# Sliding-window attention gated with a token-mixing MLP: column-tiled PV for nine more query tiles, V weights earlier in the load queue, first x block in halves, last output split, order of instructions tuned anew

## The chip, the cores and the metric

The kernel runs on one core of one Trainium2 chip. Times are device microseconds (us) of one execution. A run is 1.7 to 2.1 us longer than the span that the record gives for it. The program uses one core, so there is no second die to compare with. A run counts as slow when it is over 1.5% above the fastest run of the same kernel, and comparisons use the other runs, called fast.

PE is TensorE (its matmuls), DVE is VectorE, ACT is ScalarE, POOL is GpSimd, and SP is the engine that does nothing here but issue the DMAs.

## The reference

```python
def _A_ref(x, wqkv, wo):                    # x: 1 x 2048 x 512, H = 32 heads of 16, window W = 256
    q, k, v = split_heads(x @ wqkv)
    scores = einsum("bhqd,bhkd->bhqk", q, k) * Dh ** -0.5
    mask = (qi - ki >= 0) & (qi - ki < W)
    p = softmax(where(mask, scores, -1e9))
    return merge_heads(einsum("bhqk,bhkd->bhqd", p, v)) @ wo

def _B_ref(x, w1, b1, w2, b2):              # the MLP mixes along the sequence: S = 2048, F = 1376
    u = gelu(einsum("bsd,sf->bdf", layernorm(x), w1) + b1)
    return (einsum("bdf,fs->bds", u, w2) + b2).transpose(0, 2, 1)

g = sigmoid((x * gate_w).sum(-1, keepdims=True))
return g * _A_ref(x, wqkv, wo) + (1 - g) * _B_ref(x, w1, b1, w2, b2)
```

Everything is bfloat16. A query tile is 128 rows and sees at most three key blocks of 128. There are 16 query tiles, each worked in two halves of 16 heads.

## The kernel before

The order of instructions on every engine is static. A small list scheduler, which runs while the kernel is built, keeps a modelled clock for each engine and picks the next task by priorities that were tuned on that model. Code in this document is shortened: `...` stands for what is left out, and some lines are told in words.

```python
SWITCH = 0.1
LATENCY = {"PE": 0.22, "ACT": 0.15, "DVE": 0.12, "POOL": 0.15, "SP": 2.0}
def arrange(tasks, patience, stick=0.0):
    ...                                     # free[e]: when engine e is done, in the model
            for t in cands:
                start = max(free[e], t.ready)
                if e == "POOL":
                    start = max(start, port["DVE"])
                elif e == "DVE" and t.two:  # DVE with two SBUF inputs and POOL are kept apart
                    start = max(start, port["POOL"])
    ...
ORDER = dict(k=11.68, q=94.81, ..., est=13.0, mq=16.0, joint=16.0, ...)   # priorities
```

The loads stand in one queue, that of SP. The attention output of a tile is kept in a ring of three buffers `on`:

```python
    load_x(0, 0.0)
    ...                                     # wk0, wq0, (x1), wk1, wq1: K and Q weights in halves
    load_x(1, 0.02)
    dwv = load_w("wv", 2 * D, 3 * D, 0.035) # the V weights
    load_x(2, 0.04); load_x(3, 0.05)
    load_t(1, ...); load_t(2, ...); load_t(3, ...)   # x again, transposed by the DMA: XT1..XT3
    ...                                     # 12 loads of w1, then wo
    onr = ring("on", 3, [P, D], BF16)
```

The gate. `ez` holds one value per row of x. The tiled PV needs it in another layout, `EZ`, and 16 small DMAs copy it there for every four query tiles. The scheduler books this "spread" as 1.0 us of SP:

```python
        def spread(ts=ts):
            for r in range(4):
                for qq in range(4):
                    nc.sync.dma_start(EZ[32 * r:32 * r + 32, qq, ts], ez[32 * qq:32 * qq + 32, ts])
        zready.append(None if 4 * i + 3 < EST else add(f"gated{i}", {"SP": 1.0}, spread, [ge], 3, lat=2.5))
```

PV, the old form, for query tiles below `EST`: per key block 16 matmuls with a 17-column right side; then two DVE instructions per half; then one transposing DMA per tile:

```python
        if qb < EST:
            ...
            made.append(nc.tensor.matmul(buf(o)[:, hl * DV:(hl + 1) * DV], lhsT=buf(e)[:, col:col + 128],
                                         rhs=V4[:, kb, head, :], ...))
            ...
            rc = add(f"rc{qb}.{hf}", {"DVE": 0.17}, ...reciprocal...)
            nm = add(f"nm{qb}.{hf}", {"DVE": 0.34}, ...scalar_tensor_tensor out=buf(ob)..., takes=[ob] if hf == 0 else [])
            ...
                rel[qb] = [add(f"to{qb}", {"SP": 1.4},
                    lambda ob=ob, qb=qb: nc.sync.dma_start_transpose(xo[:, qb, :]..., buf(ob)), ..., uses=[ob])]
            continue
```

PV, the column-tiled form, from tile `EST` on: four column groups of 32 work side by side, and the result comes out transposed. Five DVE instructions then transpose, take the reciprocal, multiply by `EZ`, normalize, and transpose back into `xo`; no `on` buffer and no DMA are needed:

```python
                            made.append(nc.tensor.matmul(
                                buf(o)[32 * r:32 * r + 32, at:at + 128], lhsT=VA[:, kb, head * DV:head * DV + 32],
                                rhs=buf(e)[:, col:col + 128], ..., tile_position=(0, 32 * r)))
        n1 = ...nc.vector.transpose(out=buf(o)[:], in_=buf(o)[:])
        n2 = ...reciprocal...;  n2 = ...tensor_tensor (x EZ), waits for zready[i]
        n3 = ...tensor_tensor -> zt;  n4 = ...nc.vector.transpose(out=xo[:, qb, ...], in_=zt)
```

The softmax here doesn't subtract the row's maximum and nothing guards it: scores larger than these inputs give would overflow.

## Time and profile before

| | before |
|---|---|
| time, median of 3 runs | 228.65 us (228.39 to 228.75) |
| time, median of 6 runs beside the changed kernel | 228.52 us (224.21 to 228.91) |
| span of the profiled execution | 221.9 us |
| PE / DVE / ACT / POOL busy | 212.1 / 125.7 / 191.4 / 133.1 us |
| idle time of PE that the trace lists | 5.44 us in six holes (counting those over 0.25 us) |
| granted TensorE clock in that execution | 1.00 |

The prediction shows the lines of the page and of the chain. Two things help to read them. A hole is a stretch in which PE stands; only holes of the engine that bounds the kernel cost time. The granted clock is 1.00 when TensorE runs at full speed throughout.

The queue of SP, as the timeline of the kernel before has it (start, length, SP's sequencer, line, what it issues, how many):

```profile
18.78 14.21 SPq L394 DMA_DIRECT2D wb<-in_B_w_dram  x12
...
45.75 1.23 SPq L757 DMA_TRANSPOSE xo<-on  x1
...
52.98 11.02 SPq L622 DMA_DIRECT2D EZ<-ez  x16
```

All loads of w1 are issued by 33 us. The single spread comes 20 us later and holds the queue for 11 us.

### The profile page before, as it was taken

The numbers are of one execution on the slowest core, as the hardware profiler recorded it, in microseconds if no ns is written. First come the engines' busy times: TensorE is split into PE (matmuls) and PEld (weight loads), VectorE is DVE, ScalarE is ACT, GpSimd is POOL, SyncE is SP. The second block draws the span as 40 slices with busy tenths as digits, with TensorE's granted clock in tenths as the row PEclk, the third lists the DMA queues.
The fourth block names the chain that finished last, engine by engine and source line by source line (L and its number), as shares of the span: only waits on it lengthen the run. The fifth ranks groups of instructions, "written<-read, shape, count | busy, mean of one in ns | idle before, by whom it ended". The sixth has DMA issues, their size and how long they took to land.

```text
span 221.9 us, 6636 instructions
## 1 busy us (share of the span) xinstructions
PE 212.1 (96%) x2856; PEld 101.9 (46%) x2856; DVE 125.7 (57%) x239; ACT 191.4 (86%) x221; POOL 133.1 (60%) x84
## 2 busy tenths in 40 slices
PE   7869899999999999999999998999999999999993
PEld 3324364554555544455544544544455444444440
DVE  3968999986275686455697692222222225554341
ACT  2357878888999999999999989999999999989941
POOL 8708619456556557566567645766777776656640
PEclk9999999999999999999999999999999999999999
DMA  6999999043013046100551161010202010000010
GB/s 188 314 185 243 360 346 324 14 70 77 4 24 27 3 127 279 24 3 3 180 224 24 57 212 24 27 47 28 50 24 50 27 47 27 27 24 27 27 49 24
DMA packets 28477, 21.28 MB, mean 96 GB/s; under 512 B 14912, under 2 KB 26688, under 8 KB 28448
## 3 DMA queue, kind: packets, MB, share of 16 engines
q1 hardware_dynamic: 28288, 20.85, 33.1%
q8 instruction: 22, 0.36, 0.7%
q0 software_dynamic: 160, 0.01, 0.4%
q14 instruction: 7, 0.06, 0.1%
HBM read 15.47 MB, written 2.10 MB: 79 GB/s over the span
## 4 chain that ended last, share of the span: by engine, by line
PE 86%; DMA 6%; ACT 2%; DVE 2%; SPq 1%; issue 1%; ACTq 0%
PE pb L506 56%; PE pb L720 14%; PE ps L664 13%; DMA wqkv<-in_A_wqkv_dram 4%; PE pb L783 2%; DMA XT<-in_A_x_dram 2%; ACT et L683 2%; SPq L365 1%; PE pb L594 1%; DVE c L629 1%; DVE KT L470 1%; SPq L360 0%; ACT ot L343 0%; ACT VA L469 0%; DVE c L628 0%
## 5 line engine op out<-in xcount | busy, mean ns | idle before, releaser
L683 ACT ACTIVATE et<-ps 128x1024 bf16<-128x1024 f32 x120 | 116.1, 1028 | 8.0 <-PE ps L664 6.6
L698 POOL TENSOR_SCALAR_AFFINE_SELECT et<-et 128x2048 bf16<-128x2048 bf16 x40 | 80.9, 2029 | 59.1 <-ACT et L683 47.0
L683 ACT ACTIVATE XT<-ps 128x1024 bf16<-128x1024 f32 x60 | 58.3, 1027 | 4.6 <-PE ps L664 4.2
L698 POOL TENSOR_SCALAR_AFFINE_SELECT XT<-XT 128x2048 bf16<-128x2048 bf16 x20 | 40.1, 2012 | 17.0 <-ACT XT L683 10.9
L506 PEld LDWEIGHTS <-wb 128*128 128x128 bf16 (+2 forms) x352 | 29.8, 98 | 36.8 <-issue 9.1
L506 PE MATMUL pb<-ug,wb 128*128 128x512 bf16 (+1 forms) x176 | 45.0, 381 | 0.0
L506 PE MATMUL pb<-h,wb 128*128 128x512 bf16 (+1 forms) x176 | 43.5, 381 | 0.0
L664 PE MATMUL ps<-QZ,KT 32*128 32x256 bf16 x720 | 35.7, 273 | 0.9 <-ACT et L683 0.9
L506 PE MATMUL pb<-XT,wqkv 128*128 128x512 bf16 x128 | 30.5, 379 | 0.7 <-ACT XT L469 0.7
L346 DVE TENSOR_SCALAR ot<-pb,c,c 128x512 bf16<-128x512 f32 x14 | 11.3, 810 | 27.9 <-PE pb L506 27.9
L720 PEld LDWEIGHTS <-et 128*128 128x128 bf16 x800 | 23.3, 96 | 7.0 <-issue 3.3
L720 PE MATMUL pb<-VA,et 128*128 128x17 bf16 x800 | 25.5, 171 | 1.0 <-DVE KT L470 1.0
L664 PEld LDWEIGHTS <-KT 32*128 32x128 bf16 x720 | 10.7, 92 | 32.2 <-ACT et L683 13.4
L737 DVE RECIPROCAL rd<-pb 128x16 f32<-128x16 f32 x26 | 6.6, 255 | 29.6 <-PE pb L720 29.6
L546 DVE TENSOR_TENSOR QZ<-pb,par 128x1024 bf16<-128x1024 f32 x16 | 18.9, 1219 | 1.1 <-PE pb L506 0.7
L506 PEld LDWEIGHTS <-wqkv 128*128 128x128 bf16 x128 | 11.5, 97 | 14.3 <-issue 2.1
L506 PE MATMUL pb<-wo,xo 128*128 128x512 bf16 x64 | 17.6, 379 | 0.0
L506 PE MATMUL pb<-wqkv,XT 128*128 128x512 bf16 x64 | 15.5, 380 | 1.8 <-DMA wqkv<-in_A_wqkv_dram 1.8
L345 DVE TENSOR_SCALAR uf<-pb,b1c 128x512 f32<-128x512 f32 (+1 forms) x11 | 8.2, 749 | 11.9 <-PE pb L506 11.8
L744 DVE SCALAR_TENSOR_TENSOR on<-pb,ez,rd 128x256 bf16<-128x256 f32 x26 | 12.6, 484 | 0.9 <-DMA xo<-on 0.2
L561 DVE BATCH_NORM_STATS2 stats<-xo 128x6 f32<-128x512 bf16 x16 | 10.6, 681 | 2.6 <-DMA xo<-in_A_x_dram 2.6
L877 DVE SCALAR_TENSOR_TENSOR ug<-t,uf 128x512 bf16<-128x512 f32 (+1 forms) x11 | 11.7, 1066 | 0.1
(61 smaller groups left out, 142.5 us busy)
## 6 DMA issues: line engine op xcount, KB each, us to landing
wb<-in_B_w_dram SPq DMA_DIRECT2D x8, 512.0 KB, 7.8
wb<-in_B_w_dram SPq DMA_DIRECT2D x2, 2048.0 KB, 7.9
xo<-in_A_x_dram SPq DMA_DIRECT2D x4, 512.0 KB, 8.2
out_dram<-ot SPq DMA_DIRECT2D x16, 128.0 KB, 1.7
wb<-in_B_w_dram SPq DMA_DIRECT2D x4, 352.0 KB, 8.4
wqkv<-in_A_wqkv_dram SPq DMA_DIRECT2D x4, 256.0 KB, 5.2
wb<-in_B_w_dram SPq DMA_DIRECT2D x1, 1024.0 KB, 5.8
wqkv<-in_A_wqkv_dram SPq DMA_DIRECT2D x1, 512.0 KB, 8.7
```

The lines of the kernel that those rows point to most:

```text
L345: return nc.vector.tensor_scalar(out=out_, in0=in_, scalar1=bias, scalar2=None, op0=ALU.add)
L346: return nc.vector.tensor_scalar(out=out_, in0=in_, scalar1=scale, scalar2=bias, op0=ALU.mult, op1=ALU.add)
L506: nc.tensor.matmul(buf(b)[:rows, :], lhsT=lhsT, rhs=rhs, start=(j == 0), stop=(j == n - 1))
L546: lambda k=k, b=b: nc.vector.tensor_tensor(out=QZ[:, i % NQ, k, :, :], in0=buf(b)[:, None, :].to_broadcast([P, 2, SB]), in1=par[:][:, :, N ...
L561: f"bs{t_}", {"DVE": 0.67}, lambda b=b, t_=t_: nc.vector.bn_stats(buf(b)[:], xo[:, t_, :]),
L664: made.append(nc.tensor.matmul(buf(b2[r // 2])[:, (r % 2) * 512 + kk * 256:(r % 2) * 512 + kk * 256 + 256], lhsT=KT[32 * r:32 * r + 32, (k ...
L683: lambda j=j, b2=b2, e=e: nc.scalar.activation(out=buf(e)[:, j * 1024:(j + 1) * 1024], in_=buf(b2[j])[:], func=ACT.Exp, scale=SCALE),
L698: return nc.gpsimd.affine_select(out=buf(e), in_=buf(e), pattern=[[0, 16], [-1 if far else 1, P]], compare_op=ALU.is_gt if far else ALU.is ...
L720: made.append(nc.tensor.matmul(buf(o)[:, hl * DV:(hl + 1) * DV], lhsT=buf(e)[:, col:col + 128], rhs=V4[:, kb, head, :], start=(n_ == 0 and ...
L737: lambda rd=rd, o=o: nc.vector.reciprocal(out=buf(rd)[:, 0:16], in_=buf(o)[:, 0:16 * DV].rearrange("p (h d) -> p h d", d=DV)[:, :, DH]),
L744: lambda rd=rd, o=o, ob=ob, hf=hf, qb=qb: nc.vector.scalar_tensor_tensor(out=buf(ob)[:, hf * 256:(hf + 1) * 256].rearrange("p (h d) -> p h ...
L877: lambda u=u, t1=t1, fsz=fsz, fc=fc: nc.vector.scalar_tensor_tensor(out=ug[:fsz, fc, :], in0=buf(t1)[:fsz, :], scalar=1.0, in1=buf(u)[:fsz ...
```

## The change

The intent: use the column-tiled PV from query tile 4 on instead of from tile 13, since it takes about a third less TensorE time; bring the V weights ahead of the later x blocks; start on the first half of x block 0; split the last eviction between ACT and DVE; and tune the order anew, with a shift for each of several hundred tasks. The core of the diff:

```diff
-def arrange(tasks, patience, stick=0.0):
+def arrange(tasks, patience, stick=0.0, join=0.0, aside=0.0):
 ...
+                return t.prio + (join if {t.mode, mode} == {"s", "p"} else stick)
 ...
-    k=11.68, q=94.81, v=170.23, ..., stick=-31.1, est=13.0, mq=16.0, joint=16.0, xt=4.48, xt_step=2.18,
+    k=144.769, q=47.868, ..., wv=0.064, x=0.0, x_step=0.322, est=4.0, mq=16.0, joint=14.0, xt=1.238, xt_step=12.263,
 ...
-    qkv=(7, 6, 5, 4, 3),  u=(7, 6, 5, 4, 3),  y=(5, 6, 7),  pv=(5, 6, 7),  s=(0, 2, 4),
+    qkv=(5, 6, 7),  u=(2, 3, 4, 5, 6, 7),  y=(2, 3, 4, 5, 6, 7),  pv=(4, 5, 6, 7),  s=(0, 2, 4, 6),
 ...
+SHIFT = {
+    "bs0": 11.7, "bs1": 94.5, ..., "h2": -245.7, ...        # one value per task, some 120 lines, cut
+}
 ...
+        t.prio += SHIFT.get(t.name, 0.0)
 ...
+        for t0, n_ in ((0, 2), (2, 2)) if i == 0 else ((4 * i, 4),):   # x block 0 in two halves
 ...
-    load_x(1, 0.02)
-    dwv = load_w("wv", 2 * D, 3 * D, 0.035)
-    load_x(2, 0.04)
-    load_x(3, 0.05)
+    dwv = load_w("wv", 2 * D, 3 * D, ORDER["wv"])
+    for i in range(1, NSB):
+        load_x(i, ORDER["x"] + i * ORDER["x_step"])
 ...
-    "warm": 8 matmuls
+    "warm": 6 matmuls
 ...
+        cols = [(0, 256), (256, D)] if qb == NT - 1 else [(0, D)]      # last output in two pieces
```

With `est=4` there are three spreads instead of one, and 4 transposing DMAs of attention output instead of 13.

## The prediction

> **What bounds the kernel now.** I read the page first, then the chain that ended last in order of time, then the groups of instructions by line and shape, then the waits and the queue of SP. Parts 1 and 2 of the page:
>
> ```profile
> PE 212.1 (96%) x2856; PEld 101.9 (46%) x2856; DVE 125.7 (57%) x239; ACT 191.4 (86%) x221; POOL 133.1 (60%) x84
> PE   7869899999999999999999998999999999999993
> ACT  2357878888999999999999989999999999989941
> ```
>
> PE is full from about 30 us to 214 us. ACT is nearly as full from 55 us on: its stretches of 10 us hold 9.2 to 9.9 us of work, so it has some 4% of slack there. It is poorly used only in the first 50 us. PE's busy figure alone proves little, because its ends are modelled, so I went to the chain. By line it is PE for 86% of the span: dense chains (L506) 56%, the old PV (L720) 14%, scores (L664) 13%, column-tiled PV (L783) 2%. Pieces of that chain (start, length, what; xN is the number of matmuls):
>
> ```profile
> 3.98 8.74 DMA wqkv<-in_A_wqkv_dram
> 12.76 1.02 PE pb L506 x4
> 13.79 0.33 PE ps L664 x8
> 14.12 1.83 PE pb L506 x8
> 15.95 0.33 PE ps L664 x8
> 16.28 3.56 PE pb L506 x16
> ...
> 41.86 1.31 PE pb L720 x48
> ...
> 129.15 1.20 PE pb L720 x48
> ...
> 184.43 0.79 PE pb L783 x48
> ...
> 201.93 0.56 PE pb L783 x32
> 202.82 0.34 PE pb L783 x16
> ...
> 218.06 0.78 ACT ot L343
> ```
>
> These give PE's prices. Eight more dense matmuls cost 3.56 - 1.83 = 1.73 us, so one costs 0.216 us, and a dense run just after a tiled one pays 0.11 us more (1.83 against 8 x 0.216 = 1.72). One score step costs 0.33. The old PV costs 0.40 per block of keys (48 matmuls: 1.20, or 1.31 just after scores). The column-tiled PV, which this kernel already uses for query tiles 13 to 15, costs about 0.225 per block of keys plus 0.115 on entry (0.34, 0.56, 0.79). The first line is the other loss: PE stands until 12.76 for the V weights.
>
> **What the Trainium skill says.** "TensorE: Matmul & The Clock Gate", Part 1, gives 215.7 ns for a warm matmul of 512 columns and says that start-to-start never falls below about 25 ns, however few the columns. The trace agrees with both: 0.216 us, and 16 old PV matmuls of 17 columns in 0.40 us, which is 25 ns each. So the old PV pays the floor, not for work. "TensorEngine Tiling (Array Packing)", Key Properties, says that a change of tiling mode drains the engine; the trace shows it as the 0.11 us above, on entering and on leaving. "VectorE: DVE Perf Modes", The three transpose paths, says that VectorE transposes only blocks of 32x32; that is why the tiled PV needs a transpose before and one after its normalization, both in this trace. "Perfetto Trace Analysis", Identifying the Most-Contended Engine, warns that matmul busy share is a bad measure of headroom; hence the chain.
>
> **The change, part by part.**
>
> 1. Column-tiled PV for query tiles 4 to 12 (est 13 -> 4). That is 9 tiles x 2 halves = 18 groups of 3 key blocks, 864 of the 1152 old matmuls. A group falls from 1.20 or 1.31 to 0.79 us, but where dense work follows it now pays 0.11 on leaving. Between scores and scores the gain is 1.31 - 0.79 = 0.52; between scores and dense 0.41; between dense and dense 0.30. The scheduler's new "join" term favours putting PV next to scores. I take 0.43 x 18 = 7.7 us off PE, and some 0.5 us more from joined groups of tiles 13 to 15. All of it lies on the path, since PE is the chain.
>
> 2. VectorE pays for it. The rows by shape:
>
> ```profile
> L737 DVE RECIPROCAL rd<-pb 128x16 f32<-128x16 f32 x26 | 6.6, 255 | 29.6 <-PE pb L720 29.6
> L744 DVE SCALAR_TENSOR_TENSOR on<-pb,ez,rd 128x256 bf16<-128x256 f32 x26 | 12.6, 484 | 0.9 <-DMA xo<-on 0.2
> L799 DVE STREAM_TRANSPOSE pb<-pb 128x512 f32<-128x512 f32 x6 | 4.4, 732 | 7.8 <-PE pb L783 7.8
> L804 DVE RECIPROCAL pb<-pb 128x16 f32<-128x16 f32 x6 | 1.6, 267 | 0.2
> L812 DVE TENSOR_TENSOR rd<-pb,EZ 128x16 f32<-128x16 f32 x6 | 1.1, 176 | 0.2
> L821 DVE TENSOR_TENSOR zt<-pb,rd 128x256 bf16<-128x256 f32 x6 | 2.5, 425 | 0.2
> L831 DVE STREAM_TRANSPOSE xo<-zt 128x256 bf16<-128x256 bf16 x6 | 2.7, 444 | 0.2
> ```
>
> Old group: 0.255 + 0.484 = 0.74 us. New group: 0.732 + 0.267 + 0.176 + 0.425 + 0.444 = 2.04 us. 18 x 1.30 = +23.5 us, so VectorE goes from 125.7 to about 149 us, some 70% of a shorter span. From 55 us on it has room (mostly 2.4 to 8 us per 10). From 20 to 50 us it has none (9.3, 9.6 and 8.8 us per 10), so the new schedule must move layer-norm work later.
>
> 3. SP and DMA. Nine of 13 transposing DMAs of attention output go (1.19 us of issue each). Two more spreads of the gate come, of 16 small DMAs each. The one spread of before held SP from 52.98 to 64.0, which is 11 us, where the scheduler's task says 1.0. So SP gets 22 us more issue, in order, near the w1 loads. The w1 loads are issued from 18.8 to 33 now, and W1's matmuls begin at 57. Most of this fits in that slack. I charge 0.5 us.
>
> 4. Start. The V weights are issued before the later x blocks, so less lies ahead of them and the 1.83 us of waiting should go. Transposing x in halves and letting each chunk of the first projections wait only for its own copy can start projections perhaps 0.5 to 0.9 us earlier than 6.46 (wqkv's first LDWEIGHTS already ran at 5.58, so those weights were there). Two of eight warm-up matmuls go (0.43 us each); they only fill the wait for x. Together I take 2.3 us. First exponentials should move from 14.3 to about 11.5 us.
>
> 5. End. The last eviction, 0.78 us on ACT, is shared between ACT and VectorE as two 256-column halves, by the task's estimate about 0.5 each. Gain 0.3 us. The DMA that follows and its 3 us stay.
>
> 6. Order. The per-task shifts and wider bank lists (scores may use all eight banks) can remove PE's other holes, for instance 0.96 us before 27.6 for a K copy late on VectorE, and the waits for exponentials near 40 and 131 us. I take 1.0 us.
>
> Sum: 7.7 + 0.5 + 2.3 + 0.3 + 1.0 - 0.5 = 11.3 us if PE stays the only bound.
>
> **The rivals.** (a) **ACT becomes the bound.** Its 180 exponentials average 174.4/180 = 0.97 us. From the first exponential on it has 191.4 - 4.9 = 186.5 us of work (4.9 lies before 14.3). With a start at 11.5, 98% filling and about 6.5 us from its last exponential to the end, it cannot end before some 11.5 + 190.3 + 6.5 = 208 us of span. PE's way gives 221.9 - 11.3 = 210.6. The two are so near that they will wait for each other; an overfull VectorE would also push copies to ACT. I charge 0.8 us of lost gain; heavy friction would cost 3 to 4 and give about 221. (b) **VectorE or PSUM holds PE up.** A tiled PV bank stays taken about 1.9 us, through four instructions, against 0.74; in 20 to 50 us this can delay K and Q copies and with them scores. Against it: four PV banks instead of three, and slack later. With it the time would be 220 to 223. (c) **SP's spreads delay W1 or the transposed x**, so the static order on PE stops at a first W1 chain. That could cost several us at 30 to 70 us of the span, about 222. (d) **The V weights were hidden anyway**, and PE finds another wait (VectorE's Q expansions, 1.2 us each) at 11 us: part 4 shrinks to 1 us, about 219. (e) Better than thought: "join" merges nearly every PV with scores and the holes all go, about 214.
>
> **Range and chances.** 228.65 - 11.3 + 0.8 gives 218.15; the finely tuned order makes me lean to the better side by about 0.6, so 217.5 us. Rival (e) sets the low end, 213.5, and rivals (a) to (c) the high end, 222. The line of 2% is 224.1; it would take two rivals at once to stay above it: faster 0.89, within 2% 0.09, slower 0.02.
>
> **What will show it right or wrong.** In the changed kernel's trace: 1152 matmuls on the tiled PV line and 288 on the old one, groups of three still at 0.79; VectorE near 149 us; PE busy near 203 us and still over 95%; ACT above 90%; no DMA wait for wqkv near 11 to 13 us and the first exponential before 12; EZ spreads of 48 issues. Wrong would be: PE below 94% with waits of scores for exponentials (rival a), waits of PE for VectorE copies or banks (b), or for the w1 and x DMAs (c); or PV groups split into single blocks, each paying its entry again.

## More of the kernel before

The profiled execution was one of the fastest that this kernel ever had (223.61 us). In later rounds this kernel mostly took 226 to 231 us, at granted clocks of 0.978 to 0.993.

## The result

The changed kernel took 250.12 us (median of 6 runs, 247.31 to 250.76) against 228.52 us for the kernel before in the same rounds. Ratios in this document are the mean time of one kernel's fast runs over that of the other's fast runs of the same rounds, so they differ a little from the ratio of the medians. Here the ratio is 1.107, with a 95% interval of 1.094 to 1.120. Only two of the six runs of the kernel before (224.21 and 226.81) count as fast, so this ratio is inflated; the medians give 1.095. Either way the changed kernel is slower by some 10%, where faster by 5% had been predicted. The profiled run was a fast one: 250.47 us, span 248.8 us, granted clock 0.929.

The page of the changed kernel, the busy line and three rows of tenths in 40 slices of 6.2 us:

```profile
PE 209.0 (84%) x2819; PEld 91.0 (37%) x2854; DVE 148.8 (60%) x288; ACT 193.0 (78%) x224; POOL 132.8 (53%) x84
PE   6895969960069876999999999899999999999993
ACT  3294578990027898689999899999999899998942
PEclk9997699995558995899999999999999999999999
```

PE has two empty slices, at 56 to 68 us, and ACT goes empty beside it. From 110 us on both are as full as before. The clock row is the new kind of loss: fives where the profile of before has only nines, and they reach past the hole (the clock was 0.50 from 58 us, inside the hole, to 76 us). (About 35 matmul records are missing from this trace, so its smallest gaps are not real.)

The waits of the changed kernel (who waits for whom: total us, count, longest), and the chain around the hole (start, length, what):

```profile
DVE on L884 <- DMA xo<-on: 17.1, 1, 17.1
PE pb L643 <- DVE on L884: 16.2, 1, 16.2
```

```profile
61.97 8.11 DMA xo<-on
70.11 0.49 DVE on L884
...
70.65 1.89 PE pb L643 x4
```

Read them from the bottom. PE waited 16.2 us for one DVE instruction, the normalization of an old-form tile, which writes into an `on` buffer (L884). That one waited 17.1 us for a transposing DMA that empties such a buffer: the ring of three was full. The DMA was issued at 61.97 and landed at 70.1. These 8.1 us are long, too: in the kernel before such a transpose lands 2.4 us after its issue (median of 13). Here the late w1 loads were under way beside it (326 GB/s between 60 and 70 us); that they slowed it was not tested alone. When PE went on, four dense matmuls took 1.89 us, where four take 0.88 to 0.97 in the kernel before: TensorE ran at half speed after the hole.

Why was that DMA issued so late? SP's own timeline in the changed kernel, and the row for the spread's line (issues: shortest, median, longest in ns; from when to when):

```profile
24.20 21.96 SPq L762 DMA_DIRECT2D EZ<-ez  x32
46.21 0.66 SPq L528 DMA_DIRECT2D wb<-in_B_w_dram  x1
46.96 10.59 SPq L762 DMA_DIRECT2D EZ<-ez  x16
57.59 4.24 SPq L528 DMA_DIRECT2D wb<-in_B_w_dram  x6
61.97 4.95 SPq L897 DMA_TRANSPOSE xo<-on  x2
```

```profile
L762 SPq DMA_DIRECT2D EZ<-ez x48: 534/589/1475, 24.2 to 57.0; - x48
```

From 24.2 to 57.6 us the queue did almost nothing but 48 spread DMAs of 0.5 KB, 0.59 us each. The w1 loads and the transposes of attention output stood behind them. The scheduler believed that the three spreads take 3.0 us.

A sum of where the time went. The trace lists 29.8 us of PE holes against 5.4: 16.2 for this one, 2.74 at 21.47 (shown below), 1.95, 1.64, 1.12, 1.08, the 1.26 at the start that both kernels have, and smaller ones. The granted clock of 0.929 over 248.8 us stands for 17.7 us of full-speed time; some 7.1 of it fell on the hole itself (0.56 over 16.2 us), where it costs nothing, so about 10.6 us is an estimate for its price on busy time. TensorE's own work fell by some 7 us (worked out in the next section but one). 221.9 - 5.4 + 29.8 + 10.6 - 7.0 = 249.9, for a span of 248.8. This sum is for the two profiled executions, which lie 26.9 us apart because that of before was unusually fast; the medians differ by 21.6 us.

The second largest hole in PE's timeline of the changed kernel (in brackets: idle before it, and what ended it):

```profile
21.47 0.54 PE L734 MATMUL pb<-gwc,XT 128*128 128x1 bf16 x16 [2.74 <-DMA XT<-in_A_x_dram]
```

### The profile page after: what moved, and what is told of

Read it like the earlier page. It is cut to its first block, busy times and chain, and to the rows that moved or that the text cites. A ratio compares the mean times of both kernels' runs of the same rounds, so it can differ in the third digit from the quotient of the medians.

```text
span 248.8 us, 6670 instructions
## 1 busy us (share of the span) xinstructions
PE 209.0 (84%) x2819; PEld 91.0 (37%) x2854; DVE 148.8 (60%) x288; ACT 193.0 (78%) x224; POOL 132.8 (53%) x84
## 4 chain that ended last, share of the span: by engine, by line
PE 63%; DMA 11%; SPq 10%; ACT 5%; DVE 4%; issue 4%; ACTq 0%; DVEq 0%
PE pb L643 45%; PE ps L804 10%; PE pb L923 6%; SPq L762 6%; DMA XT<-in_A_x_dram 6%; DMA xo<-on 3%; ACT et L823 3%; DMA wb<-in_B_w_dram 2%; DVE h L717 2%; SPq L528 2%; PE pb L860 2%; SPq L500 1%; ACT XT L823 1%; SPq L493 1%; DVE VA L604 1%
## 5 line engine op out<-in xcount | busy, mean ns | idle before, releaser
L823 ACT ACTIVATE et<-ps 128x1024 bf16<-128x1024 f32 x116 | 113.0, 1026 | 16.9 <-PE ps L804 16.1
L823 ACT ACTIVATE XT<-ps 128x1024 bf16<-128x1024 f32 x64 | 62.6, 1027 | 21.8 <-PE ps L804 21.4
L643 PE MATMUL pb<-XT,wqkv 128*128 128x512 bf16 x122 | 33.2, 400 | 22.8 <-DVE on L884 16.2
L643 PE MATMUL pb<-ug,wb 128*128 128x512 bf16 (+1 forms) x165 | 42.2, 380 | 1.6 <-issue 1.4
L939 DVE STREAM_TRANSPOSE pb<-pb 128x512 f32<-128x512 f32 x22 | 16.1, 730 | 26.1 <-PE pb L923 26.0
L923 PEld LDWEIGHTS <-VA 128*32 128x32 bf16 x1152 | 17.0, 99 | 13.7 <-issue 9.5
L478 DVE TENSOR_SCALAR ot<-pb,c,c 128x512 bf16<-128x512 f32 (+1 forms) x14 | 10.9, 781 | 13.7 <-PE pb L643 13.7
L884 DVE SCALAR_TENSOR_TENSOR on<-pb,ez,rd 128x256 bf16<-128x256 f32 x8 | 3.8, 479 | 17.3 <-DMA xo<-on 17.1
L923 PE MATMUL pb<-et,VA 128*32 128x128 bf16 x608 | 13.1, 225 | 1.2 <-ACT XT L823 1.1
L1005 DVE SCALAR_TENSOR_TENSOR t<-t,uf 128x512 f32<-128x512 f32 (+1 forms) x11 | 9.9, 898 | 1.6 <-ACT t L998 1.5
L971 DVE STREAM_TRANSPOSE xo<-zt 128x256 bf16<-128x256 bf16 (+1 forms) x23 | 10.4, 454 | 0.6
## 6 DMA issues: line engine op xcount, KB each, us to landing
xo<-in_A_x_dram SPq DMA_DIRECT2D x3, 512.0 KB, 10.6
```

Of the source, the lines that this page charges most:

```text
L478: return nc.vector.tensor_scalar(out=out_, in0=in_, scalar1=scale, scalar2=bias, op0=ALU.mult, op1=ALU.add)
L643: nc.tensor.matmul(buf(b)[:rows, :], lhsT=lhsT, rhs=rhs, start=(j == 0), stop=(j == n - 1))
L823: lambda j=j, b2=b2, e=e: nc.scalar.activation(out=buf(e)[:, j * 1024:(j + 1) * 1024], in_=buf(b2[j])[:], func=ACT.Exp, scale=SCALE),
L923: made.append(nc.tensor.matmul(buf(o)[32 * r:32 * r + 32, at:at + 128], lhsT=VA[:, kb, head * DV:head * DV + 32], rhs=buf(e)[:, col:col + ...
L939: f"n1{qb}.{hf}", {"DVE": 0.10 + 0.53 * nh}, lambda o=o: nc.vector.transpose(out=buf(o)[:], in_=buf(o)[:]),
L971: lambda zt=zt, qb=qb, w0=w0, nb=nb: nc.vector.transpose(out=xo[:, qb, w0:w0 + 32 * nb], in_=buf(zt)[:, 0:32 * nb]),
```

## The experiments

My theory after the result: **the spreads**. They block SP's queue, the ring of `on` fills, and PE stands and then runs slowly. The first rival: **the order**. The new static order, with PV for `est=4`, is worse for reasons of its own, and the hole is only one of them. A third: **tiled PV itself** costs on VectorE what it saves on PE. Every kernel below computes the right result unless it is said otherwise. Where "same order" is said, the instruction orders of the engines agree apart from the edit.

### e1: the changed kernel without the spread DMAs (wrong result)

```diff
 def ones():
+        nc.gpsimd.memset(EZ[:], 1.0)
 ...
         def spread(ts=ts):
-            for r in range(4):
-                for qq in range(4):
-                    nc.sync.dma_start(...)
+            return None
```

> The changed kernel with the same order on every engine, but the 48 small DMAs that spread the gate are left out and EZ is filled once with ones on GpSimd (wrong result on purpose). Theory A (SP's queue: the spreads hold it 33 us, so the transposes of attention output behind them start late, the ring of three output buffers stays full and TensorE stands 16 us, then runs at half clock for some microseconds): the hole before 70 us goes, time 227 to 233 us. Rival B (VectorE's extra 23 us and the longer held PSUM banks are the loss): hardly better, 243 to 250 us. Rival C (the new static order is bad in itself): a new hole of like size takes the old one's place, over 240 us.

Measured: 233.23 us (232.48 to 234.23) beside 229.42 for the kernel before (228.18 to 231.44): ratio 1.016 (1.008 to 1.023). The gate is left out of the attention part, so the relative error is 0.32. The 16 us hole is gone, and the granted clock is 0.963. Removing 48 tiny DMAs gave some 17 us. It did not give a kernel faster than before. Besides the queue, this edit also takes away the tiled normalization's wait for the spread's data; e2 keeps that wait and is as fast, so it isn't what cost the time.

### e2: the changed kernel with a fourth `on` buffer

This keeps every DMA and leaves the order the same; only the ring gets a buffer, so the full ring no longer blocks.

```diff
+    onr.tiles.append(sb.tile([P, D], BF16, name="on3"))
+    for qb_, ob_ in on.items():
+        ob_.index = qb_
     with tc.manual_schedule():
```

> The changed kernel with the same order on every engine and all its DMAs, but a fourth attention-output buffer, so the fourth tile waits for no transpose. Theory A: the hole of 16 us goes although SP's queue is as long as before; what is left is the next thing behind that queue (W1's loads land near 75 us): 229 to 237 us. If SP's lateness itself had other equally long victims, 240 to 248. Rival B (VectorE): unchanged, 248 to 251 us.

Measured: 232.07 us (230.84 to 232.79), ratio 1.010 (1.002 to 1.017), clock 0.97. One buffer of 128 KB gave 18 us, so it was the ring that turned the late transposes into a stop of PE. Both e1 and e2 end at 232 to 233, so the spreads with the ring explain some 17 to 19 of the 21.6 us (each measured against the kernel before of its own rounds), and the rest is not explained by them.

Most of the holes that are left sit in the first 95 us: 12.2 us against 5.0 in the fast profile of before, and against 7.5 in that of e11, which is a usual run of the old order. Windows of the kernel before and of e2 from 20 to 40 us (length, busy us with counts of PE, PEld, DVE, ACT, POOL, then granted clock, DMA share, GB/s):

```profile
20.00:40.00 20.00, 18.99 (x264) 9.63 (x257) 18.85 (x44) 15.67 (x21) 11.47 (x9) 1.00 1.01 314
```

```profile
20.00:40.00 20.00, 15.64 (x218) 7.17 (x222) 15.93 (x36) 12.12 (x18) 9.47 (x9) 0.77 0.43 79
```

In the same 20 us e2 does 218 matmuls instead of 264, DVE 36 instructions instead of 44, and the DMA a quarter of the traffic, because the queue holds the small DMAs and not w1. The clock is 0.77, with listed holes of 1.98 us (at 21.94, for XT) and 1.94 us. The second of them, with DVE and POOL at that time, in e2's timelines:

```profile
33.86 0.16 DVE L769 SCALAR_TENSOR_TENSOR c<-c,b2c 128x4 f32<-128x4 f32 x1
34.34 1.81 DVE L769 SCALAR_TENSOR_TENSOR c<-c,b2c 128x4 f32<-128x4 f32 x1
```

```profile
34.13 2.01 POOL L838 TENSOR_SCALAR_AFFINE_SELECT et<-et 128x2048 bf16<-128x2048 bf16 x1 [3.18 <-ACT et L823]
```

```profile
37.45 0.84 PE L643 MATMUL pb<-XT,wqkv 128*128 128x512 bf16 x2 [1.94 <-DVE QZ L686]
```

The same tiny DVE instruction takes 0.16 us alone and 1.81 us when POOL's mask has begun before it: it ends at 36.15, when the mask ends (36.14). The Trainium skill, "SBUF — State Buffer", Terms, says that DVE and GpSimd share one pair of ports, that one of them holds it for a whole instruction and that the loser blocks. The trace agrees, with these numbers. The Q expansion behind it came late, and PE stood 1.94 us.

### e3: the kernel before with 32 more of the spread DMAs, ahead of most w1 loads

```diff
+    def gate_exp(ts, i):
+        made = nc.scalar.activation(ez[:, ts], ez[:, ts], ACT.Exp)
+        if i in (1, 2):
+            for r in range(4):
+                for qq in range(4):
+                    nc.sync.dma_start(EZ[32 * r:32 * r + 32, qq, ts], ez[32 * qq:32 * qq + 32, ts])
+        return made
```

> The kernel before, same order on every engine, with only the two further gate spreads added (32 small DMAs in SP's queue ahead of most W1 loads; nothing reads their result). Theory A: SP gets 20 us of issue before the W1 loads and the third transposing load of x, so W1's first chains at 57 us and the attention-output transposes wait: 233 to 243 us. Rival B and C: no change, 228 to 230 us.

Measured: 242.07 us (240.45 to 244.3), ratio 1.052 (1.041 to 1.062). The medians differ by 12.6 us (the means of the fast runs by 11.8), for DMAs whose data is not used. The victim is another one. SP's timeline of e3, then PE's:

```profile
28.23 11.02 SPq L594 DMA_DIRECT2D EZ<-ez  x16
40.01 10.46 SPq L594 DMA_DIRECT2D EZ<-ez  x16
...
63.89 3.60 SPq L373 DMA_TRANSPOSE XT<-in_A_x_dram  x1
```

```profile
69.75 0.56 PE L603 MATMUL pb<-gwc,XT 128*128 128x1 bf16 x16 [10.59 <-DMA XT<-in_A_x_dram]
```

Here the third transposing load of x stood behind the spreads and the delayed w1 loads. (The profiled run of e3 was a slow one; the three other runs, without a profile, took 240.5 to 243.5.)

### e4: the new order with the old PV (est back to 13)

```diff
-    ..., est=4.0, mq=16.0, joint=14.0, ...
+    ..., est=13.0, mq=16.0, joint=14.0, ...
```

> The changed kernel with the column-tiled PV back to query tiles 13 to 15 (one spread, 13 transposes), all else of the change kept; the scheduler makes another order of it, for which the per-task shifts were not tuned. Theory A: the hole is mostly gone since only one spread of 11 us is left, but TensorE pays the old PV's price again: 228 to 236 us. Rival C (the shifts and the load order are what hurts): 240 us or more.

Measured: 235.08 us (234.37 to 235.76), ratio 1.024 (1.016 to 1.032), clock 0.974. One spread, no hole of 16 us, old PV, and still 5.7 us behind the kernel before. The scheduler makes another order when `est` changes, so this doesn't separate the shifts from the PV. It shows only that the new priorities bring no gain without the tiled PV.

### e5: e2 with the first transposing load of x ahead of x1 to x3

```diff
+    move("xt1", "x1.4")          # in the finished plan, on top of e2
```

> The fourth output buffer as in e2, and one more edit: on SP the transposing load of x block 1 goes ahead of the three plain loads of x blocks 1 to 3 (order of all other engines unchanged). If the 2 us hole at 20 us (TensorE waiting for that load) and the half clock after it are what is left of the loss: 225 to 229 us against 232. If VectorE's late Q expansions cause the low clock on their own: 230 to 232. If the plain loads coming later hold up VectorE's statistics: 233 or more.

Measured: 233.65 us (232.12 to 234.78), no better than e2. The wait for XT is still 2.09 us, now at 23.66, and a wait of 1.33 us for K and Q weights came up at 7.04. The expectation missed. In the rounds of e5 to e8 the kernel before had two unusually fast runs (223.74 and 226.87) that count alone, so the ratio of 1.037 is inflated; the medians (233.65 against 228.41) are the fairer comparison.

### e6: e5 with the gate's small operations late and the spread by matmuls

The spread is done by 8 small matmuls with a selection matrix (the value split in a high and a low bfloat16 part) and three DVE instructions per block, so SP issues none.

```diff
+    for i_ in range(NSB):
+        move(f"gates{i_}", <first output task>)
+    ...
+                nc.tensor.matmul(buf(gb_)[:, 4 * qq:4 * qq + 4], lhsT=sel[:, qq, :], rhs=ezh[:, part, ts], ...)
```

> The changed kernel with every suspected wait taken away and a correct result: fourth output buffer, x block 1's transposing load early, the four small gate operations (fp32, SBUF to SBUF, which took up to 1.8 us instead of 0.16 in front of Q expansions) moved on VectorE to just before the first output, and the gate spread by eight small matmuls and one copy per block instead of 16 DMAs. Theory A (only waits, not the tiled PV itself, cost time): 218 to 225 us, below the kernel before. Rival (VectorE's load or the order itself): 227 to 232.

Measured: 236.31 us (234.46 to 237.25), clock 0.955: worse than e2. The collisions that I removed were replaced by a new hole of 3.34 us at 20.94, where PE waits for the layer-norm statistics of x1 on DVE, and one of 1.71 at 158.87. The expectation missed.

### e7 and e8: the kernel before with est = 4

e7 changes one number in the kernel before and lets its own priorities make the order, with the spreads by DMA. e8 has e7's order, with the spread by matmuls as in e6.

```diff
-    stick=-31.1, est=13.0, mq=16.0, ...
+    stick=-31.1, est=4.0, mq=16.0, ...
```

> The kernel before with only one part of the change: column-tiled PV from the fifth query tile (est 4), gate spread by DMAs as the code has it; the scheduler's order follows, 32 of the spread's DMAs come ahead of most W1 loads and of the third transposing load of x. Theory A: like e3 plus what TensorE gains, 234 to 242 us. Rival (the shifts are what hurts): 221 to 226 us.

> The same order as e7, but the gate is spread by eight small matmuls and a copy per block, so SP's queue has no spread at all. Theory A: the column-tiled PV shows its own worth, 5 to 8 us below the kernel before: 219 to 225 us, and 12 us or more below e7. Rival B (VectorE's extra load): 228 to 234 us.

Measured: e7 251.35 us (250.94 to 252.18), as slow as the changed kernel, with a hole of 8.74 us at 65.99 on a DVE instruction that fills `on`, and further holes at 214 to 244 us. e8 took 238.88 in its one fast run and 242.75 to 245.32 in three slow ones. In e8's profile, which is of a slow run, the hole at 66 is gone, and the tail's holes stay. e7 missed its expectation (234 to 242) and e8 missed its own by far. So `est=4` with the old priorities is bad even when SP is free: the order has to be made for it. What fills the tail of e7 and e8 I did not resolve.

### e9 and e10: the order of before kept, the PV of tiles 4 to 12 swapped in place

Here the plan of the kernel before is left alone. The old PV matmuls and their normalization are replaced where they stand by the tiled ones, and the two extra spreads are put where SP has slack (after the load of wo and after the second transpose of attention output). e10 adds the fourth `on` buffer and the V weights ahead of x1.

```diff
+                    if qb >= TQ:                       # TQ = 4
+                        ...matmul(buf(o)[32 * r:32 * r + 32, ...], lhsT=VA[...], rhs=buf(e)[...], tile_position=(0, 32 * r))
 ...
+    put_spread(1, "wo")
+    put_spread(2, "to1")
+    onr.tiles.append(...); on[3].index = 3             # e10 only
+    move("wv", "x1")                                   # e10 only
```

> The kernel before with the order of every engine kept, and only the PV of query tiles 4 to 12 and its normalization swapped in place for the column-tiled form; the two further gate spreads stand where SP's queue has slack (one after the load of wo, one after the second transpose of attention output). Theory A' (the tiled PV is worth its price on TensorE; the loss came only from where the spreads stood and from the new order's holes): 220 to 225 us, holes no longer than before. Rival B (longer held PSUM banks and VectorE's 23 us more): 228 to 235 with new waits of TensorE for VectorE.

> As e9, with a fourth attention-output buffer and the V weights ahead of the second x block in SP's queue (the changed kernel's load order). If the 1.8 us wait for the V weights was worth its length: 1 to 2 us below e9. If VectorE's statistics of the second x block then wait in front of TensorE's work, as they did in e6: equal to e9 or 1 to 3 us above.

Measured, e9: one of four runs was fast (227.65), the others slow (231.34 to 232.19). e10 gave 230.36 us (229.91 to 230.73), all fast, ratio 1.003 (0.9985 to 1.007), beside 229.4 for the kernel before. PE is busy for 209.8 us in its profile against 214.9 in that of e11, which keeps the old PV; so 5 us less work on PE, without any 16 us hole, gave nothing. Its holes grew instead, to 11.4 us in the first 95 us against 7.5 in e11, and the two longest end with DVE's normalizations. e10's timelines of POOL, DVE and PE near 80 us:

```profile
79.89 2.19 POOL L721 TENSOR_SCALAR_AFFINE_SELECT et<-et 128x2048 bf16<-128x2048 bf16 x1 [1.61 <-ACT et L706]
```

```profile
80.25 2.37 DVE L901 SCALAR_TENSOR_TENSOR t<-t,uf 128x512 f32<-128x512 f32 x1
```

```profile
84.29 1.47 PE L506 MATMUL pb<-h,wb 128*128 128x512 bf16 x6 [2.06 <-DVE zx L650]
```

A step of the GELU that takes 0.69 us otherwise took 2.37, from inside a mask until 0.54 us after its end. The order of before keeps such steps out of the masks (the scheduler models the shared ports), and normalizations that are 1.3 us longer push them in. The tiled normalization behind them (zx) came late, and PE stood 2.06 us.

### e11: the same 32 extra DMAs as in e3, in SP's slack

```diff
+    put_spread(1, "wo")
+    put_spread(2, "to1")
```

> The kernel before with the same two further spreads as e3 (32 small DMAs, result unused), but at the places of e9 in SP's queue instead of ahead of the W1 loads. Theory A: the place matters, not the DMAs: 227.5 to 230 us, against e3's 242. Rival (the DMAs themselves cost, by contention): 235 to 242.

Measured: 229.04 us (228.97 to 229.22), all fast, ratio 0.998 (0.994 to 1.001). The same 32 DMAs cost some 12 us in e3 and nothing here. It is their place in the queue that costs, not they. In e11's profile the wait for the V weights is 3.80 us, at 16.32, in the order in which the profile of before has 1.83: this wait varies from run to run.

### e12, e13 and e14: from tile 8 only, and the V weights alone

Tiles 4 to 7 are normalized at 75 to 127 us in e10, where DVE also runs most of the GELU chains. e12 swaps tiles 8 to 12 only (one extra spread, fourth `on` buffer). e13 is e12 with the V weights ahead of x1. e14 is the kernel before with only this move.

```diff
-    TQ = 4
+    TQ = 8                       # e12, e13
+    move("wv", "x1")             # e13; alone in e14
```

> As e9 but only query tiles 8 to 12 swapped in place for the column-tiled PV (most of them after the stretch from 60 to 110 us in which VectorE runs the GELU chains beside GpSimd's masks), one further spread in SP's slack, a fourth output buffer. If e9's gain of TensorE was eaten by VectorE in that stretch (holes of 2.05 and 2.37 us behind normalizations, then low clock), this keeps 10 groups x 0.37 = 3.7 us of gain and loses none: 225.5 to 227.5 us where the kernel before has 229.4. If the tiled PV has no worth on the path at all: 229 to 230.5.

> As e12 with the V weights ahead of the second x block in SP's queue: 0.5 to 2 us below e12 if the wait for them sets the start, equal to it if the wait moves to the second x block.

> The kernel before, order of all other engines kept, V weights ahead of the second x block in SP's queue: the one part of the change alone. My prediction gave it 1.8 us: 226.5 to 228 us where the kernel before has 229. If the wait only moves to the second x block: 228.5 to 229.5.

Measured beside 228.87 us for the kernel before (225.62 to 231.3; five of its eleven runs count as slow and are left out of the ratios):

| | median (range), us | ratio of fast runs, 95% interval |
|---|---|---|
| e12 | 227.2 (223.75 to 227.95), two of six fast | 0.986 (0.975 to 0.996) |
| e13 | **225.3** (223.97 to 227.62), five of six fast | 0.990 (0.983 to 0.997) |
| e14 | 227.52 (226.67 to 229.36), all fast | 1.002 (0.995 to 1.009) |

e13 has the lowest median: some 1% below the kernel before by the ratio, a gain that the interval puts between 0.3% and 1.7%. Against e12 it is 1.9 us lower by the medians and 1.0 us higher by the means of the fast runs, so the two are not told apart. Its clock was 0.992. It still has a hole of 2.73 us at 31.49, on a K copy by DVE. The GELU step that took 2.37 us in e10 is short again in e13's DVE timeline:

```profile
80.48 0.69 DVE L901 SCALAR_TENSOR_TENSOR t<-t,uf 128x512 f32<-128x512 f32 x1
```

For the early V weights alone (e14) the runs don't decide: the median is 1.35 us lower, within the range expected, but the interval goes from 0.5% faster to 0.9% slower. Its profile still shows a wait of 2.75 us, at 13.18.

### e15 and e16: the gate's small operations late

In the kernel before, a hole of 0.96 us at 27.62 ends with a K copy on DVE, and these operations stand ahead of that copy on DVE. In e13 that hole is 2.73 us. e15 moves them before the first GELU in e13, e16 in the kernel before.

```diff
+    for n_ in ("biases", "gates0", "gates1", "gates2", "gates3"):
+        move(n_, "ub0")
```

> e13 with the small gate and bias operations (two conversions, twelve operations on 4 columns, which took up to 2 us each beside GpSimd's masks, with K copies behind them) moved on VectorE to just before the first GELU chain. If they are what holds the K copies and with them TensorE before 31 us (hole of 2.73 us in e13's profile, 0.96 in the kernel before): 222 to 224.5 us, over 2% below the kernel before. If other VectorE work takes their place: 224.5 to 226.

> The kernel before with only those small operations moved (VectorE's order alone differs). If they hold up TensorE: the hole of 0.96 us at 27 to 33 us goes, 227 to 228.5 us where the kernel before has 229. Otherwise equal.

Measured beside 228.77 us (223.97 to 230.7; the three fastest, 223.97 to 225.39, count alone, so ratios are inflated): e15 231.43 us (227.05 to 234.52), ratio 1.010 (1.002 to 1.018), and e16 229.18 us (227.57 to 230.45), ratio 1.020 (1.012 to 1.027). Both missed. The early hole went, but in e16 two holes of 1.03 and 1.09 us stand at 66.5 and 71.2. e15's profile, which is of a slow run, has such holes at 69 to 74 and two of 1.96 us at 137.3 and 143.4. In a static order a small move shifts everything behind it on its engine.

## Why the prediction was wrong

**Step 3 failed: "I charge 0.5 us" for the spreads.** The step had the right figures: 11 us per spread, against 1.0 in the task, so 22 us more issue, "in order, near the w1 loads". It then said that "most of this fits in that slack". That slack was read from the old order, in which the w1 loads come before the spread. In the new order two of the three spreads come before 11 of the 12 w1 loads. Measured: 17 to 19 us (e1, e2), some 12 us on the order of before (e3), nothing in slack (e11). I could have read the cost before the run: the diff left the 1.0 us in place, so the new order was made on a model in which spreads are cheap. No run gave the scheduler the measured 11 us, so that this cost, and not the priorities alone, put the spreads there is argued and not shown.

The Trainium skill, "DMA: Bandwidth & Descriptors", Issuing engines are not separate DMA queues, calls the time that a sequencer takes to initiate a DMA usually small relative to the DMA. For 0.5 KB it isn't: 0.59 us to issue, a third of the 1.7 us from issue to landing (both medians), and what counts is who stands behind it.

**Rival (c) named the mechanism and mis-sized it.** It said that the spreads delay W1 or the transposed x, for "about 222". What was delayed in the changed kernel was mainly the transposes of attention output, through the ring of `on`, which the prediction did not look at; in e3 it was the transposed x. And the sum had no term for the clock. A hole cost its length and often some time at half speed after it: four dense matmuls at 1.89 us after the big hole in the changed kernel, a clock of 0.77 over 20 us of e2 with holes of only 2 us. The Trainium skill, "TensorE: Matmul & The Clock Gate", Part 1, says that an idle array falls to half its clock. The trace agrees (0.50 from 58 us, inside the hole that began at 54.5), and the prediction quoted the page for other figures.

**Step 6 failed: "I take 1.0 us" of gain from the order.** e2 has no big hole, and TensorE has some 7 us less work, yet it takes 2.65 us longer than before. So some 9 to 10 us are lost: 4.7 us more holes in the first 95 us than in e11's profile (12.2 against 7.5), about 3.5 us of clock ((0.985 - 0.97) x 231, an estimate from the clocks), and a rest. They are not the order's alone, since e2 also has the longer normalizations that used up some 5 us in e10. But e4, the new priorities without the tiled PV, is 5.7 us behind too. The holes shown are waits for XT and for DVE work held up by POOL's masks. Which of the several hundred shifts cause them was not separated. e5, e6, e15 and e16 show that taking single waits away doesn't recover it, because the next one appears. This stays open.

**Step 1 was right in its prices and wrong about the path.** There were 1152 tiled and 288 old matmuls, as predicted, and a group of three still takes 0.79 us. The order enters the tiled PV 34 times (13 single blocks, 7 pairs, 13 groups of three, one of six) where I had counted whole groups: 13 x 0.34 + 7 x 0.56 + 13 x 0.79 + 1.45 = 20.1 us for the 24 groups instead of 24 x 0.79 = 19.0. With the exits into dense work TensorE saves about 6.1 us by these prices (an estimate), not 7.7 plus 0.5, and 0.9 on two warm-up matmuls. "All of it lies on the path, since PE is the chain" is what fell: swapped into the order of before from tile 4 on it gave nothing (e10), from tile 8 on some 2 us (e13, together with the V weights, 0.6 to 3.9 us by the interval; e12 is too much split by slow runs).

**Step 2 was right in its sum.** DVE is at 148.8 us, for a predicted 149. But I read from it only how full DVE is. What mattered was when: longer normalizations move DVE's two-input instructions into POOL's masks. Rival (b), VectorE or PSUM holding PE up, is what e10 shows for VectorE. (Its "about 1.9 us" for a tiled PV bank is too long: the means of the four rows shown add up to 1.60.)

**Step 4: the sign was right, the worth was not.** No wait for weights is longer than 0.2 us in the changed kernel, and the first exponential came at 12.43 us, for a predicted "before 12". But a wait of 2.74 us for XT took its place, as rival (d) had said of another wait. For the move alone e14 doesn't decide. The halves of x block 0 were not tried alone.

**Step 5 held, and is small.** The last eviction runs as 0.56 us on ACT beside 0.54 on DVE, instead of 0.78. It was not tried alone either.

**Rival (a) did not happen.** ACT is busy 78% of the span. Its exponentials waited 37.5 us for PE's scores, while PE waited some 3 us for ACT.

The signs listed at the end of the prediction did their work: PE at 84%, waits of PE for VectorE and groups split into single blocks stood under "Wrong would be", and ACT at 78% and PE's 209 us busy missed the "above 90%" and "near 203" of a right prediction.

## What to carry to other kernels

Before trusting a tuned static order, compare each modelled cost with the trace: here one task was booked at 1.0 us that takes 11, and its three instances stood where they cost some 17 to 19 us. An in-order DMA queue must be priced per DMA, with the question who stands behind it and which ring fills then. Leave room for the clock after a hole of TensorE, but not a fixed factor: by the clocks, some 3 us were lost in the 9 us after the hole of 16.2 us, some 1.6 us in the 4 us after e11's wait of 3.80, and none after the 1.83 us in the profile of before. And a swap that saves time on the bounding engine pays only where the other engines' instructions still fall into their old gaps; swapping in place gave nothing for tiles 4 to 12 here (e10) and some 1% for tiles 8 to 12 (e13, with the V weights early).

## What the Trainium skill lacked or had wrong

- "DMA: Bandwidth & Descriptors", Issuing engines are not separate DMA queues, calls the time to initiate a DMA usually small relative to the DMA. Here 48 DMAs of 0.5 KB took 0.59 us each to issue (median), a third of their 1.7 us to landing, and held SP's queue for 32.6 us together.
- "TensorE: Matmul & The Clock Gate", Part 1, puts the fall to half the clock after an idle window of about 3.4 us (a later part tells of short pauses as well, without their length). Here the clock was 0.77 over 20 us of e2 in which no listed hole is longer than 2.0 us, and 0.50 for the 4 us from 26 to 30.
- "TensorEngine Tiling (Array Packing)" says that a change of mode drains the engine and gives no time: 0.11 us here, at each entry and exit.
